# Moving the small transfers of a grouped-query attention backward kernel from POOL's DMA queue to the sync engine's

## The chip, the cores and the metric

The kernel runs on one core of a Trainium2 chip. The metric is the device time of one execution in microseconds (us). Every run used here was in the fast state, with a mean granted TensorE clock of 0.98 to 1.00 except where a text says otherwise. Engines: PE multiplies matrices, DVE and ACT work on vectors, POOL is the general engine, and SP is the sync engine, which here only issues transfers. In the traces a transfer issued by SP or ACT stands in a hardware DMA queue (q1, q10), one issued by POOL in the software one (q0). A ring is the list of transfers that such a queue has on one DMA engine. A transfer lands when the last of its completion signals has come.

## The reference

Forward and backward of softmax attention, 32 batches, 32 query heads on 4 key heads, 4 queries, 2048 keys, head size 128, bf16.

```python
def _fwd_reference(q, k, v):               # q 32x32x4x128, k and v 32x4x2048x128
    k = jnp.repeat(k, Hq // Hkv, axis=1); v = jnp.repeat(v, Hq // Hkv, axis=1)
    scores = jnp.einsum("bhqd,bhkd->bhqk", q, k) * D ** -0.5
    return jnp.einsum("bhqk,bhkd->bhqd", _softmax(scores), v)

def reference(q, k, v, grad_out):
    out, vjp = jax.vjp(_fwd_reference, q, k, v)
    return (out, *vjp(grad_out))           # out, dq, dk, dv
```

Per batch this is 2 MB each of k, v, dk and dv, and 32 KB each of q, grad_out, out and dq.

## The kernel before

The work of a batch is cut into units. A table gives each unit a planned time; units are sorted by it, and each engine runs its own in that order. The names that matter: LQ loads q and grad_out; LK and LV load k and v in transfers of 1 MB; DVs and DKs store dv and dk, 1 MB each; Os and DQs store out and dq; Oe and DQe are the copies that make out and dq in SBUF; QT and VT are PE's transposes of q and v.

```python
PERIOD = 21.3
PLACE = dict(LQ=[-47.936], LK=[-16.977, -14.467], LV=[3.599, 0.95], QT=[-7.484], ...  # cut
    Oe=[18.672], Os=[94.455], DQe=[52.911], DQs=[136.569], ...)                        # cut
SHIFT = {0: dict(LQ=[-769.808], ..., DQs=[-81.021], ...), ...}   # first and last batches; cut
# planned time of a unit: b * PERIOD + PLACE[name] + SHIFT
...
    sm_pool = pool("small", 4)              # four buffers for each name: q, go, o, dq, ...
...
        if name == "LQ":
            t["q"] = sm_pool.tile([P, D], BF16, name="q_sb")
            nc.gpsimd.dma_start(out=t["q"][:], in_=q_r[b])
            t["go"] = sm_pool.tile([P, D], BF16, name="go_sb")
            nc.gpsimd.dma_start(out=t["go"][:], in_=go_r[b])
        elif name in ("LK", "LV"):
            ...                             # cut; 1 MB a transfer
                nc.sync.dma_start(out=whole[:, h], in_=src[b, g][:, h])
...
        elif name in ("Oe", "DQe"):
            x, by = ("o", "rinv") if name == "Oe" else ("dq", "rs")
            t[x] = sm_pool.tile([P, D], BF16, name=x + "_sb")
            ...                             # cut; on ACT or DVE
        elif name in ("Os", "DQs"):
            nc.gpsimd.dma_start(out=(o_r if name == "Os" else dq_r)[b], in_=t["o" if name == "Os" else "dq"][:])
...
        elif name in ("DVs", "DKs"):
            nc.sync.dma_start(...)          # cut; 1 MB a transfer
```

Of the kernel before, what the change touches and what calls it, by code (L numbers as in the profile page):

```python
# [278 lines left out]
def kernel(  # L279
# [11 lines left out]
    nc = tc.nc  # L291
# [25 lines left out]
    q_r, go_r, o_r, dq_r = rows(q), rows(grad_out), rows(out_0), rows(out_1)  # L317
# [12 lines left out]
    def bank(b, *what, n=1, dt=FP32):  # L330
        i = bank_of[(b, "ps", what[0], n) + what[1:]]
        x = psum[:, QW * i:QW * (i + n)]
        return x if dt is FP32 else x.bitcast(BF16).rearrange("p (c d) -> p c d", d=P)

    def copy16(on, out, in_):
        if on == "ACT":
            nc.scalar.copy(out=out.rearrange("p c d -> p (c d)").bitcast(FP32),  # L337
                           in_=in_.rearrange("p c d -> p (c d)").bitcast(FP32))
        else:
            nc.vector.tensor_copy(out=out, in_=in_)  # L340

    def emit(u):
        b, name, arg = u.key[0], u.key[1], u.key[2:]
        t = T[b]
        if name == "LQ":
            t["q"] = sm_pool.tile([P, D], BF16, name="q_sb")
            nc.gpsimd.dma_start(out=t["q"][:], in_=q_r[b])
            t["go"] = sm_pool.tile([P, D], BF16, name="go_sb")
            nc.gpsimd.dma_start(out=t["go"][:], in_=go_r[b])
        elif name in ("LK", "LV"):  # L350
            g, = arg
            p_, src = (k_pool, k_r) if name == "LK" else (v_pool, v_r)
# [79 lines left out]
        elif name in ("ETe", "DTe"):  # L432
            copy16(u.on, t[(name[:2],) + arg][:], t[(name[:2] + "p",) + arg][:])
        elif name in ("O", "DQ"):
            i, = arg
            if i == 0:
                t[name] = bank(b, name)
            xt, x = ("ET", "V") if name == "O" else ("DT", "K")
            for c in range(4 * i, 4 * i + 4):
                for h in range(NH):  # L440
                    r = slice(32 * h, 32 * h + 32)
                    nc.tensor.matmul(t[name][r, 0:D], lhsT=t[xt, c // 8][:, c % 8, r], rhs=t[x, h][:, c, :],  # L442
                                     start=(c == 0), stop=(c == C - 1), tile_position=(0, 32 * h))
# [3 lines that stand above are left out]
            src = t[name[:-1]][:, 0:D]  # L447
            if u.on == "ACT":
                nc.scalar.activation(out=t[x][:], in_=src, func=ACT.Copy, scale=t[by][:])
            else:  # L450
                nc.vector.tensor_scalar(out=t[x][:], in0=src, scalar1=t[by][:], scalar2=None, op0=ALU.mult)
        elif name in ("Os", "DQs"):
            nc.gpsimd.dma_start(out=(o_r if name == "Os" else dq_r)[b], in_=t["o" if name == "Os" else "dq"][:])
        elif name == "DL":
            t["dl"] = sm_pool.tile([P, 1], FP32, name="delta")
            nc.vector.tensor_tensor_reduce(out=junk[:], in0=t["o"][:], in1=t["go"][:], scale=1.0, scalar=0.0,
                                           op0=ALU.mult, op1=ALU.add, accum_out=t["dl"][:])
        elif name == "DS":
            i, = arg
            if i == 0:  # L460
                t["ds"] = ds_pool.tile([P, Sk], BF16, name="ds_sb")
            w = slice(2 * QW * i, 2 * QW * i + 2 * QW)
            nc.vector.scalar_tensor_tensor(out=t["ds"][:, w], in0=t["DP", i][:], scalar=t["dl"][:],  # L463
                                           in1=t["e"][:, w], op0=ALU.subtract, op1=ALU.mult)
        elif name in ("DV", "DK"):
            i, = arg
            if i == 0:
                for g in range(2):
                    t[name, "out", g] = o_pool.tile([P, 2, C, D], BF16, name=name.lower() + "_sb", tag="out")
            accs = [bank(b, name, i, g, n=2) for g in range(2)]  # L470
            t[name, i] = accs
            lhs, rhs = ("e", "dop") if name == "DV" else ("ds", "qp")
            for j in range(CPQ):
                c = CPQ * i + j
                for g in range(2):
                    r = slice(64 * g, 64 * g + 64)
                    nc.tensor.matmul(accs[g][:, 2 * P * j:2 * P * j + 2 * P], lhsT=t[lhs][r, P * c:P * c + P],  # L477
                                     rhs=t[rhs][r, :, :].rearrange("p h d -> p (h d)"), start=True, stop=True,
                                     tile_position=(64 * g, 0))
        elif name in ("DVe", "DKe"):  # L480
            i, g = arg
            copy = nc.scalar.copy if u.on == "ACT" else nc.vector.tensor_copy
            copy(out=t[name[:2], "out", g][:, :, CPQ * i:CPQ * i + CPQ, :],  # L483
                 in_=t[name[:2], i][g][:].rearrange("p (c h d) -> p h c d", h=2, d=D))
        elif name in ("DVh", "DKh"):
            g, w = arg
            c = slice(C // 2 * w, C // 2 * w + C // 2)
            nc.sync.dma_start(out=(dv_r if name == "DVh" else dk_r)[b, g].rearrange("p h (c d) -> p h c d", d=D)[:, :, c],
                              in_=t[name[:2], "out", g][:, :, c, :])
        elif name in ("DVs", "DKs"):  # L490
            g, = arg
            nc.sync.dma_start(out=(dv_r if name == "DVs" else dk_r)[b, g],
                                in_=t[name[:2], "out", g][:].rearrange("p h c d -> p h (c d)"))

    with tc.manual_schedule():
        for u in order:
            if u.on or not u.eng:
                emit(u)
# [27 lines left out]
```

## Time and profile before

| | before |
|---|---|
| median of 2 runs, us | 693.48 (693.37 to 693.58) |
| span of the profiled run, us | 688.6 |
| PE, DVE, ACT, POOL busy | 90%, 81%, 88%, 30% |
| large transfers, issue to landing, 300 to 600 us | 18.7 to 20.6 us |
| small transfers, the same | 5.7 to 6.2 us |

Such a profile is read from what is never idle. Here these are the 16 DMA engines, and the number to look at next is not how busy a queue is, but how long a transfer waits in it. The lines stand in the prediction below.

### The profile page before, as it was taken

The numbers are of one execution on the slowest core, as the hardware profiler recorded it, in microseconds if no ns is written. First come the engines' busy times: TensorE is split into PE (matmuls) and PEld (weight loads), VectorE is DVE, ScalarE is ACT, GpSimd is POOL, SyncE is SP. The second block draws the span as 40 slices with busy tenths as digits, with TensorE's granted clock in tenths as the row PEclk, the third lists the DMA queues.
The fourth block names the chain that finished last, engine by engine and source line by source line (L and its number), as shares of the span: only waits on it lengthen the run. The fifth ranks groups of instructions, "written<-read, shape, count | busy, mean of one in ns | idle before, by whom it ended". The sixth has DMA issues, their size and how long they took to land.

```text
span 688.6 us, 28403 instructions
## 1 busy us (share of the span) xinstructions
PE 620.1 (90%) x12352; PEld 467.1 (68%) x12352; DVE 558.3 (81%) x776; ACT 604.4 (88%) x921; POOL 208.8 (30%) x426
## 2 busy tenths in 40 slices
PE   5899999999999999999999899998889998989984
PEld 4677677777677777766667666676666766766753
DVE  3788888888889888888788878787787887888885
ACT  2889999999999999998899888899888998888883
POOL 2423321333322233331233321333212333113330
PEclk9999999999999999999999999999999999999998
DMA  9999999999999999999999999999999999999967
GB/s 347 403 413 387 415 414 409 415 415 416 415 416 416 414 416 412 397 407 413 408 409 405 410 412 414 399 398 412 405 412 405 406 401 397 408 403 386 391 260 263
DMA packets 75005, 274.47 MB, mean 399 GB/s; under 512 B 6272, under 2 KB 6272, under 8 KB 74880
## 3 DMA queue, kind: packets, MB, share of 16 engines
q1 hardware_dynamic: 70784, 268.45, 97.6%
q0 software_dynamic: 4096, 4.20, 1.8%
q8 instruction: 96, 1.57, 0.8%
q14 instruction: 29, 0.24, 0.1%
HBM read 136.31 MB, written 136.31 MB: 396 GB/s over the span
## 4 chain that ended last, share of the span: by engine, by line
DMA 55%; PE 22%; ACT 13%; issue 5%; POOL 3%; DVE 2%; SPq 0%; POOLq 0%; DVEq 0%; ACTq 0%
DMA v_sb<-in_v_dram 52%; PE psum L372 10%; PE psum L477 6%; ACT dk_sb L483 4%; ACT dv_sb L483 4%; PE psum L431 3%; DMA out_dram<-dv_sb 2%; ACT e_sb L399 2%; PE psum L442 2%; ACT vt_sb L337 2%; POOL dop_sb_103 L411 1%; PE psum L383 1%; DVE kt_sb L390 1%; ACT kt_sb L337 1%; DMA go_sb<-in_grad_out_dram 1%
## 5 line engine op out<-in xcount | busy, mean ns | idle before, releaser
L483 ACT CAST dk_sb<-psum 128x1024 bf16<-128x1024 f32 x159 | 157.6, 1013 | 25.9 <-PE psum L477 24.5
L483 ACT CAST dv_sb<-psum 128x1024 bf16<-128x1024 f32 x155 | 151.7, 1022 | 13.2 <-PE psum L477 12.4
L372 PE MATMUL psum<-ident,v_sb 128*128 128x128 bf16 x2048 | 147.4, 220 | 16.8 <-DMA v_sb<-in_v_dram 15.3
L372 PEld LDWEIGHTS <-v_sb 128*128 128x128 bf16 x2048 | 117.9, 98 | 56.9 <-issue 32.8
L372 PE MATMUL psum<-ident,k_sb 128*128 128x128 bf16 x2048 | 142.4, 221 | 10.2 <-ACT dk_sb L483 10.2
L372 PEld LDWEIGHTS <-k_sb 128*128 128x128 bf16 x2048 | 121.4, 99 | 27.1 <-issue 24.3
L483 DVE CAST dv_sb<-psum 128x1024 bf16<-128x1024 f32 x101 | 122.8, 1220 | 10.8 <-PE psum L477 10.6
L483 DVE CAST dk_sb<-psum 128x1024 bf16<-128x1024 f32 x97 | 115.9, 1219 | 8.5 <-ACT kt_sb L337 4.5
L337 ACT COPY kt_sb<-psum 128x512 f32<-128x512 f32 x190 | 110.3, 595 | 6.6 <-PE psum L372 5.1
L411 POOL TENSOR_SCALAR dop_sb_103<-go_sb,rinv 32x128 bf16<-32x128 bf16 x64 | 38.5, 602 | 225.4 <-DVE rinv L404 97.3
L411 POOL TENSOR_SCALAR dop_sb_102<-go_sb,rinv 32x128 bf16<-32x128 bf16 x64 | 38.5, 602 | 212.5 <-DVE rinv L404 141.1
L463 DVE SCALAR_TENSOR_TENSOR ds_sb<-psum,delta,e_sb 128x1024 bf16<-128x1024 f32 x64 | 81.9, 1279 | 15.1 <-ACT vt_sb L337 13.5
L337 ACT COPY vt_sb<-psum 128x512 f32<-128x512 f32 x131 | 75.5, 599 | 17.6 <-PE psum L372 16.6
L340 DVE COPY vt_sb<-psum 128x1024 bf16<-128x1024 bf16 x125 | 82.9, 681 | 2.9 <-PE psum L372 2.6
L477 PEld LDWEIGHTS <-e_sb 64*128 64x128 bf16 x1024 | 50.0, 93 | 36.3 <-issue 19.6
L399 ACT ACTIVATE e_sb<-psum,m 128x1024 bf16<-128x1024 f32 x64 | 71.1, 1122 | 2.4 <-DVE kt_sb L390 2.2
L340 DVE COPY kt_sb<-psum 128x1024 bf16<-128x1024 bf16 x66 | 44.9, 685 | 18.8 <-PE psum L372 18.8
L477 PEld LDWEIGHTS <-ds_sb 64*128 64x128 bf16 x1024 | 43.3, 94 | 23.8 <-issue 8.8
L477 PE MATMUL psum<-dop_sb_103,e_sb 64*128 64x256 bf16 x512 | 45.2, 270 | 4.1 <-POOL dop_sb_103 L411 1.6
L477 PE MATMUL psum<-dop_sb_102,e_sb 64*128 64x256 bf16 x512 | 44.9, 270 | 3.2 <-ACT dv_sb L483 0.7
L390 DVE TENSOR_SCALAR_CACHE_REDUCE kt_sb<-psum 128x1024 bf16<-128x1024 f32 x32 | 39.2, 1225 | 9.6 <-issue 7.7
L390 DVE TENSOR_SCALAR_CACHE_REDUCE kt_sb<-psum,m 128x1024 bf16<-128x1024 f32 x32 | 41.1, 1284 | 6.5 <-DVE kt_sb L390 3.9
(83 smaller groups left out, 764.5 us busy)
## 6 DMA issues: line engine op xcount, KB each, us to landing
k_sb<-in_k_dram SPq DMA_DIRECT2D x62, 1024.0 KB, 18.7
v_sb<-in_v_dram SPq DMA_DIRECT2D x62, 1024.0 KB, 19.6
out_dram<-dv_sb SPq DMA_DIRECT2D x62, 1024.0 KB, 19.0
out_dram<-dk_sb SPq DMA_DIRECT2D x62, 1024.0 KB, 18.8
k_sb<-in_k_dram SPq DMA_DIRECT2D x4, 512.0 KB, 5.4
v_sb<-in_v_dram SPq DMA_DIRECT2D x4, 512.0 KB, 9.4
out_dram<-dv_sb SPq DMA_DIRECT2D x4, 512.0 KB, 7.9
out_dram<-dk_sb SPq DMA_DIRECT2D x4, 512.0 KB, 6.7
```

The costliest lines, as they stand in the source:

```text
L337: nc.scalar.copy(out=out.rearrange("p c d -> p (c d)").bitcast(FP32), in_=in_.rearrange("p c d -> p (c d)").bitcast(FP32))
L340: nc.vector.tensor_copy(out=out, in_=in_)
L372: nc.tensor.transpose(out=ps[:, j, :], in_=t[x, h][:, 8 * i + j, :], identity=ident[:])
L383: nc.tensor.matmul(t[name, i][r, QW * w:QW * w + QW], lhsT=t["qdt"][:, side, r], rhs=t[x, h, i][:, CPQ * w:CPQ * w + CPQ, :], start=True, ...
L390: nc.vector.tensor_scalar(out=spent, in0=t["S", i][:], scalar1=-scale, scalar2=t["m"][:] if i else None, op0=ALU.mult, op1=ALU.min, accum_ ...
L399: nc.scalar.activation(out=t["e"][:, 2 * QW * i:2 * QW * i + 2 * QW], in_=t["S", i][:], func=ACT.Exp, bias=t["m"][:], scale=scale, accum_o ...
L411: nc.gpsimd.tensor_scalar(out=t["dop"][r, h % 2, :], in0=t["go"][r, :], scalar1=t["rinv"][r, :], scalar2=None, op0=ALU.mult)
L431: nc.tensor.transpose(out=ps[:, j, :], in_=src[:, P * c:P * c + P], identity=ident[:])
L442: nc.tensor.matmul(t[name][r, 0:D], lhsT=t[xt, c // 8][:, c % 8, r], rhs=t[x, h][:, c, :], start=(c == 0), stop=(c == C - 1), tile_positio ...
L463: nc.vector.scalar_tensor_tensor(out=t["ds"][:, w], in0=t["DP", i][:], scalar=t["dl"][:], in1=t["e"][:, w], op0=ALU.subtract, op1=ALU.mult)
L477: nc.tensor.matmul(accs[g][:, 2 * P * j:2 * P * j + 2 * P], lhsT=t[lhs][r, P * c:P * c + P], rhs=t[rhs][r, :, :].rearrange("p h d -> p (h ...
L483: copy(out=t[name[:2], "out", g][:, :, CPQ * i:CPQ * i + CPQ, :], in_=t[name[:2], i][g][:].rearrange("p (c h d) -> p h c d", h=2, d=D))
```

## The change

The intent is to rid POOL of issuing transfers, and to send everything by the hardware path.

```diff
         if name == "LQ":
             t["q"] = sm_pool.tile([P, D], BF16, name="q_sb")
-            nc.gpsimd.dma_start(out=t["q"][:], in_=q_r[b])
+            nc.sync.dma_start(out=t["q"][:], in_=q_r[b])
             t["go"] = sm_pool.tile([P, D], BF16, name="go_sb")
-            nc.gpsimd.dma_start(out=t["go"][:], in_=go_r[b])
+            nc.sync.dma_start(out=t["go"][:], in_=go_r[b])
...
         elif name in ("Os", "DQs"):
-            nc.gpsimd.dma_start(out=(o_r if name == "Os" else dq_r)[b], in_=t["o" if name == "Os" else "dq"][:])
+            nc.sync.dma_start(out=(o_r if name == "Os" else dq_r)[b], in_=t["o" if name == "Os" else "dq"][:])
```

## The prediction

> **What bounds the kernel now.** I read, in this order, the strip of 40 slices, the DMA queues, the chain that ended last, the waits, then the timeline of the queues around 400 us, at the start and at the end.
>
> ```profile
> DMA  9999999999999999999999999999999999999967
> q1 hardware_dynamic: 70784, 268.45, 97.6%
> q0 software_dynamic: 4096, 4.20, 1.8%
> DMA 55%; PE 22%; ACT 13%; issue 5%; POOL 3%; DVE 2%; SPq 0%; POOLq 0%; DVEq 0%; ACTq 0%
> ```
>
> The 16 DMA engines are busy in all but the last two slices, and over half of the last chain is DMA. So **transfers bound the kernel**, not an engine: a batch (21.1 us from 276 us on) moves eight transfers of 1 MB on the sync queue (q1) and four of 32 KB on POOL's queue (q0). What decides is how long each waits in its queue, over 300 to 600 us:
>
> ```profile
> v_sb<-in_v_dram SPq DMA_DIRECT2D x29, 1024.0 KB, 20.6
> out_dram<-dk_sb SPq DMA_DIRECT2D x28, 1024.0 KB, 18.9
> ...
> q_sb<-in_q_dram POOLq DMA_DIRECT2D x14, 32.0 KB, 5.9
> ...
> out_dram<-dq_sb POOLq DMA_DIRECT2D x14, 32.0 KB, 6.2
> ```
>
> The last number is us from issue to landing. A 1 MB transfer takes about 2.6 us of all engines (256 packets of 4 KB, 160 to 164 ns each in the packet records, over 16), so 19 us is a whole batch of transfers queued ahead. The small ones pass that backlog in 6 us, because they stand in another queue. That is what the change takes away.
>
> **What the Trainium skill says.** "DMA: Bandwidth & Descriptors", section "Issuing engines are not separate DMA queues": transfers of all issuers run on the same 16 engines. The trace agrees: packet by packet, at least 16 are active at any time from 100 us on, and when a q0 packet runs, fewer q1 packets do. So the small transfers already cost DMA time, and moving them frees none. Same page, "Queues, rings and completion order": an engine takes turns between rings, and consumes one ring in order. The 6 against 19 us agree. "Perfetto Trace Analysis", section "DMA Instruction — HWDGE (DVE, Sync)": a sync-queue issue waits for its semaphores in the sequencer before it starts, so later issues wait behind it. The first page's "SWDGE vs HWDGE vs iDMA" calls the hardware path the faster to set up; here that matters only where the queue is empty, which it hardly ever is.
>
> **The change, part by part.**
>
> *POOL.* It loses 128 issues of about 0.57 us, 73 us of its 208.8. It is idle 70% of the span; all waits of matmuls on its dop tiles come to 1.6 us. Worth nothing.
>
> *Sync queue, issue.* It gains 128 issues. The program's order per batch b becomes: dv stores, v loads, k load, dk stores, k load, **dq store of b-4, out store of b-2**, q and grad_out loads. The issues already use eight semaphores in turn, and each waits for the landing of the one eight before it: eight in flight at most, exactly one batch today. With twelve per batch, eight in flight are still at least 3 to 5 MB, 8 to 13 us of work, so this limit alone should not empty the engines.
>
> *The order put into the queue.* Both small tiles have four buffers, so the ACT copy that makes dq of b+4 waits until dq of b is stored.
>
> ```profile
> 414.64 0.60 POOL L453 DMA_DIRECT2D out_dram<-dq_sb  x1
> 416.31 2.62 SPq L358 DMA_DIRECT2D k_sb<-in_k_dram  x1
> 423.47 0.37 ACT L449 ACTIVATE dq_sb<-psum,rs 128x128 bf16<-128x128 f32 x1
> ```
>
> Today that store is issued at 414.6 and lands 6.5 us later, 2.4 us before its buffer is needed at 423.5. In the changed order it stands behind the k load, issued until 418.9 and landing about 435.2: 11.7 us late. The same sum gives 5 us late when it first bites (about 196 us), 12 us late from 290 us on. **I do not expect 12 us per batch.** A stalled ACT makes everything later once; then the compute runs that much closer behind the DMA engines, which keep working off the queue, and the pace stays theirs. A check: after the copy, ACT needs 8.8 us until the next dk stores are ready (423.5 to 432.3); behind the dq store stand dv stores, v loads and a k load, 5 MB or 13 us, so the engines do not run dry, with 1 to 2 us to spare. What remains is what the lag costs at the end.
>
> *The end.* The order there puts the last q load (batch 31) directly behind the last v load.
>
> ```profile
> 638.06 4.57 SPq L358 DMA_DIRECT2D v_sb<-in_v_dram  x1
> 650.81 0.22 PE L361 MATMUL psum<-ident,q_sb 128*128 128x128 bf16 x1
> 656.48 0.62 PE L372 MATMUL psum<-ident,v_sb 128*128 128x128 bf16 x8 [1.13 <-DMA v_sb<-in_v_dram]
> ```
>
> That v load lands 20.9 us after issue, at 658.9. The transpose of q, at 650.8 now, must wait for it: 8.1 us. PE waits 1.1 us for v anyway at 656.5, so the end moves by **+7 us**. The lag of the dq stores at this point (7.3 us for batch 23's) is the same time, not an addition.
>
> *The start.* dq of batch 0 is ready only when ACT has made it, yet its store stands ahead of the second dk store:
>
> ```profile
> 41.11 1.25 SPq L492 DMA_DIRECT2D out_dram<-dk_sb  x2
> 48.47 1.29 SPq L492 DMA_DIRECT2D out_dram<-dv_sb  x2
> ...
> 51.58 0.43 ACT L449 ACTIVATE dq_sb<-psum,rs 128x128 bf16<-128x128 f32 x1
> ```
>
> The sync engine would stand from 42.8 to 52.0 us. The backlog is small then: the first dk store lands at 48.9. The other dk store and two dv stores (3 MB) come after 52 instead of 42 and 48.5; the second dk would land at about 59 (52, plus 1.7 for the issues before it, plus 5 for one transfer through an empty queue), the dv stores at 61.5 and 64, the next v load at 66.5 instead of 60.8. From there the engines are full to the end, so the hole is not made good: **+5.7 us**. At the very start q arrives earlier and k 0.8 us later; I count nothing.
>
> *The packets.* Packet records of before: 4 B (a semaphore) 9 ns, 2048 B 84, 4096 B 159. So time is about 9 ns plus 37 ns per KB. Today POOL's queue moves a small transfer in 16 packets of 2 KB, one an engine, 84 ns. The sync queue's packets have the size of one row's piece (4096 and, in the last stores, 2048 B), so I expect 256 B packets, eight an engine: an estimate of 8 x 18.4 = 147 ns. That is +63 ns x 128 = **+8 us**. If they are merged, 0; if short packets cost 30 ns, +20.
>
> *The rate.* 4 KB packets average 160.4 ns from 140 to 260 us, but 162 to 165 from 276 on, with eight always in flight. If fewer MB in flight brings back the lower figure, 2% of 345 us, 6.5 us, returns. I see no cause in the trace, so I take half: **-3 us**.
>
> Sum: 693.5 + 7 + 5.7 + 8 - 3 = 711.2, so **711 us**.
>
> **The rivals.** (1) *Hidden anyway, or a gain*: POOL's work goes, the packets are merged, the rate gets better, the hole at the start closes: 693 to 700. For it: POOL's issues are real work, DMA bytes do not change. Against: POOL bounds nothing, and the backlog of 19 us is plain. (2) *The dq wait recurs each batch*: if its loop (copy, 8.8 us of ACT, issue, 3 MB, landing; together about 20.3 us) turns out longer than the DMA's 21 us, the engines run dry 1 us or more a batch for 24 batches: 735 or more. Against: my sum is 0.7 us under; but that is thin, and gives the range its upper side. (3) *Only the end counts*: packets merged, start covered: 700.
>
> **Range and chances.** Packets (0 to 20), start (3 to 7), end (4 to 9), rate (-6 to 0), dry spells (0 to 8) do not err together: 701 to 725 holds it 8 times in 10. 2% slower begins at 707.3, below my centre but inside the errors of packets and rate: slower 0.69, within 2% 0.29, faster 0.02.
>
> **What would show it.** dq's ACT copy waits for the dq store from about 190 us on, some 10 us the first times together, then under 1 to 2 us a batch; small transfers take 8 to 14 us to land; 1 MB ones fall from 19 to 10 to 14. The wait on v disappears until the end. Sync waits for dq of batch 0 until about 52 us and the DMA strip has a dent there. PE waits for the last q some 8 us, near 660. q1 has 16384 packets of 256 B more. Wrong would be: packets of 2 KB on q1, dents in the DMA strip in mid-run, or a last batch that makes up the lag.

## The result and the profile after

The changed kernel takes **711.59 us** (710.53 to 712.64, 2 runs) against 693.48: a ratio of 1.0274, with a 95% interval of 1.0211 to 1.0337. The ratio is the recorded one, from the fast runs of both kernels in the same rounds; the quotient of the two times shown is 1.0261, so the change costs 18 to 19 us, and with two runs the interval reaches from 14.6 to 23.4. The span of the profiled run went from 688.6 to 708.8 us.

The page of the changed kernel, the DMA strip and its rate in slices of 17.7 us, and the queues:

```profile
DMA  8979999999999999999999999999999999999958
GB/s 335 402 299 344 403 415 412 414 416 415 413 409 367 405 403 404 401 395 400 402 402 391 407 391 400 405 406 394 398 396 397 405 367 383 413 397 415 358 187 324
DMA packets 89341, 274.47 MB, mean 387 GB/s; under 512 B 22656, under 2 KB 22656, under 8 KB 89216
q1 hardware_dynamic: 89216, 272.65, 98.2%
```

The bytes are the same. There are 16384 more packets under 512 B than the 6272 of before: 256 B each, as forecast. The dent is in slices 3 and 4 (35 to 71 us), and there is a small one in slice 13 (213 to 230 us). How long transfers wait, over 300 to 600 us (count, KB, us to landing):

```profile
out_dram<-dk_sb SPq DMA_DIRECT2D x28, 1024.0 KB, 8.7
...
v_sb<-in_v_dram SPq DMA_DIRECT2D x28, 1024.0 KB, 10.7
out_dram<-dq_sb SPq DMA_DIRECT2D x14, 32.0 KB, 11.2
...
q_sb<-in_q_dram SPq DMA_DIRECT2D x13, 32.0 KB, 8.9
```

A small transfer now waits as long as a large one, and the large ones wait half as long as before: the prediction's reason, that the compute runs closer behind and less stands in the queue, is not measured by itself.

The 19 us of before are not a backlog that stands in front of all engines. The trace has 16 completion signals for each transfer, and a landing is the last of them. For the 1 MB transfers from 300 to 600 us the first signal came a median 7.4 us after issue and the last 19.1; 7.4 us of this the last one came alone, behind the other 15. After the change the first came after 6.8 us, and the last 3.9 us later. So nearly all of the shorter wait is that the 16 signals come closer together; why one ran so far behind was not looked into.

The first long wait, in the timeline of ACT (start us, duration us, engine, line, operation, and in brackets the idle time before and what ended it):

```profile
197.17 1.01 ACT L483 CAST dk_sb<-psum 128x1024 bf16<-128x1024 f32 x1 [0.86 <-PE psum L477]
207.64 0.37 ACT L449 ACTIVATE dq_sb<-psum,rs 128x128 bf16<-128x128 f32 x1 [9.45 <-DMA out_dram<-dq_sb]
```

ACT stands 9.5 us at the copy of dq of batch 7 until the store of dq of batch 3 has landed. In the whole run such waits come to 18.6 us in 8 places: one long one, then little ones. At the start, in the timeline of SP:

```profile
41.14 0.38 SPq L492 DMA_DIRECT2D out_dram<-dk_sb  x1
42.80 0.36 SPq L453 DMA_DIRECT2D out_dram<-o_sb  x1
52.06 0.34 SPq L453 DMA_DIRECT2D out_dram<-dq_sb  x1
...
53.41 1.19 SPq L492 DMA_DIRECT2D out_dram<-dk_sb  x1
```

SP stands from 43.2 to 52.1 us before the first dq store, and the second dk store, which was issued at 42 us before, goes out at 53.4. Busy times and rate from 34 to 54 us, of the kernel before and of the changed one, in this order (the last two columns are the busy share of the DMA engines, which can pass 1 where packets overlap, and GB/s):

```profile
34.00:54.00 20.00, 18.40 (x375) 13.73 (x373) 17.43 (x25) 17.91 (x29) 6.37 (x13) 1.00 1.02 412
```

```profile
34.00:54.00 20.00, 18.40 (x376) 13.73 (x373) 17.41 (x25) 17.90 (x29) 4.17 (x9) 1.00 0.74 297
```

The DMA engines lose 28% of 20 us, 5.6 us, while PE, DVE and ACT are as busy as before. At the end, the timelines of SP and PE, one line of each:

```profile
654.20 2.41 SPq L347 DMA_DIRECT2D q_sb<-in_q_dram  x1
...
670.53 0.23 PE L361 MATMUL psum<-ident,q_sb 128*128 128x128 bf16 x1 [1.25 <-DMA q_sb<-in_q_dram]
```

The last q load lands 16.3 us after issue, right behind the last v load, and PE transposes q at 670.5 instead of 650.8.

Two times, read from the trace of each run against the kernel before, tell the causes apart: when the second v load of batches 3 and 31 lands (where the stream of transfers stands), and when dq of batch 31 is copied (where the compute stands). The second minus the first, at batch 31, is called the lag below. In the changed kernel they are +7.7, +11.4 and +18.4 us; the span is +20.2. So 7.7 us are lost before batch 3, 3.7 more by the stream up to batch 31, 7.0 by the compute behind it, and 1.8 after that.

A third figure is the time of the 4 KB packets over their usual 159 ns, summed and divided by 16 engines: the **excess**. It was 17.2 us before and is 21.7 us now. It is a mean over the engines, while a transfer lands with its last signal, so it is a hint and not a price.

Two limits of these figures: each is from one trace, and the trace of the kernel before was a quick execution, with a span of 688.6 us where the timed runs beside the experiments had 689.4 to 692.9. Differences against before that are read from traces can so be some 1 to 4 us too high; compare the runs with each other.

### The profile page after: what moved, and what is told of

It reads as the page before. It is cut to its first block, busy times and chain, and to the rows that moved or that the text cites. A ratio compares the mean times of both kernels' runs of the same rounds, so it can differ in the third digit from the quotient of the medians.

```text
span 708.8 us, 28450 instructions
## 1 busy us (share of the span) xinstructions
PE 626.2 (88%) x12352; PEld 473.1 (67%) x12352; DVE 560.2 (79%) x776; ACT 601.4 (85%) x921; POOL 131.9 (19%) x298
## 4 chain that ended last, share of the span: by engine, by line
PE 44%; ACT 24%; DMA 19%; issue 5%; DVE 4%; POOL 2%; SPq 1%; ACTq 0%; DVEq 0%; POOLq 0%
PE psum L372 19%; DMA out_dram<-dq_sb 14%; PE psum L477 12%; ACT dk_sb L483 9%; PE psum L431 7%; ACT dv_sb L483 5%; ACT e_sb L399 5%; DMA q_sb<-in_q_dram 4%; PE psum L442 3%; ACT vt_sb L337 3%; PE psum L383 2%; DMA v_sb<-in_v_dram 2%; POOL dop_sb L411 2%; DVE kt_sb L390 1%; SPq L358 1%
## 5 line engine op out<-in xcount | busy, mean ns | idle before, releaser
L411 POOL TENSOR_SCALAR dop_sb<-go_sb,rinv 32x128 bf16<-32x128 bf16 x128 | 76.4, 597 | 541.1 <-PE psum L431 405.3
L372 PE MATMUL psum<-ident,v_sb 128*128 128x128 bf16 x2048 | 152.3, 221 | 19.8 <-ACT dq_sb L449 17.8
L372 PEld LDWEIGHTS <-v_sb 128*128 128x128 bf16 x2048 | 120.4, 99 | 61.1 <-issue 54.5
L477 PE MATMUL psum<-dop_sb,e_sb 64*128 64x256 bf16 x1024 | 88.9, 271 | 7.4 <-DVE dv_sb L483 1.5
L477 PE MATMUL psum<-qp_sb,ds_sb 64*128 64x256 bf16 x1024 | 81.1, 271 | 2.4 <-DVE ds_sb L463 1.3
L477 PEld LDWEIGHTS <-e_sb 64*128 64x128 bf16 x1024 | 50.2, 93 | 35.1 <-issue 17.5
L419 POOL TENSOR_SCALAR qp_sb<-q_sb,rinv 32x128 bf16<-32x128 bf16 x128 | 46.9, 366 | 10.5
L431 PE MATMUL psum<-ident,ds_sb 128*128 128x128 bf16 x512 | 39.1, 220 | 10.7 <-ACT e_sb L399 10.7
```

Of the source, the lines that this page charges most:

```text
L372: nc.tensor.transpose(out=ps[:, j, :], in_=t[x, h][:, 8 * i + j, :], identity=ident[:])
L411: nc.gpsimd.tensor_scalar(out=t["dop"][r, h % 2, :], in0=t["go"][r, :], scalar1=t["rinv"][r, :], scalar2=None, op0=ALU.mult)
L419: nc.gpsimd.tensor_scalar(out=t["qp"][r, h % 2, :], in0=t["q"][r, :], scalar1=t["rinv"][r, :], scalar2=scale, op0=ALU.mult, op1=ALU.mult)
L431: nc.tensor.transpose(out=ps[:, j, :], in_=src[:, P * c:P * c + P], identity=ident[:])
L477: nc.tensor.matmul(accs[g][:, 2 * P * j:2 * P * j + 2 * P], lhsT=t[lhs][r, P * c:P * c + P], rhs=t[rhs][r, :, :].rearrange("p h d -> p (h ...
```

## The experiments

Each was a correct kernel, run with three rounds beside the kernel before on the same chip (three chips in all); differences in us come from the ratio times 693. The change itself was timed in another session, with two runs, and an interval of 14.6 to 23.4 us: differences of a few us from it are not clear of noise.

| run | ratio, 95% interval | us over before | v of batch 3 | v of batch 31 | dq of batch 31 | excess, us |
|---|---|---|---|---|---|---|
| the change | 1.0274 (1.0211 to 1.0337) | 19.0 | +7.7 | +11.4 | +18.4 | 21.7 |
| dq_only | 1.0165 (1.0139 to 1.0191) | 11.4 | +5.7 | +9.2 | +15.8 | 22.0 |
| lq_only | 1.0199 (1.0162 to 1.0236) | 13.8 | -0.3 | +5.9 | +15.7 | 19.7 |
| o_only | 1.0025 (1.0008 to 1.0042) | 1.7 | -1.3 | +1.3 | +1.3 | 17.5 |
| start_order | 1.0182 (1.0153 to 1.0211) | 12.6 | +0.6 | +6.1 | +14.7 | 22.6 |
| end_order | 1.0251 (1.0220 to 1.0281) | 17.4 | +8.3 | +13.5 | +18.6 | 23.1 |
| dq6_bufs | 1.0220 (1.0192 to 1.0248) | 15.2 | +9.4 | +7.8 | +14.9 | 17.2 |
| end_both | 1.0087 (1.0064 to 1.0110) | 6.0 | +8.6 | +8.1 | +8.2 | 16.2 |
| all_fixes | 1.0060 (1.0038 to 1.0082) | 4.2 | -0.2 | +5.7 | +5.7 | 20.7 |
| extra_loads | 1.0178 (1.0151 to 1.0205) | 12.3 | +0.6 | +15.7 | +15.7 | 24.3 |
| dq_fixed | 0.9963 (0.9948 to 0.9978) | -2.6 | -0.3 | +0.9 | +0.9 | 18.1 |

### One part of the change at a time

`dq_only`, from the kernel before:

```diff
-            nc.gpsimd.dma_start(out=(o_r if name == "Os" else dq_r)[b], ...)
+            (nc.gpsimd if name == "Os" else nc.sync).dma_start(out=(o_r if name == "Os" else dq_r)[b], ...)
```

> Only the dq stores go to the sync queue; the out stores and the q and grad_out loads stay with POOL. My theory: the hole at the start is due to the first dq store alone (+7.5 us on the landing of the loads from batch 3 on, as in the full change), 32 transfers in short packets cost 32 x 63 ns = +2 us, and the wait of ACT for the dq store puts the compute some 5 to 6 us closer behind the DMA engines at the end: 693.5 + 7.5 + 2 + 5.5 = 708.5 us. Rival A (the end is late only because the last q load stands behind the last v load): no lag at the end, 703 us. Rival B (the loads or out stores make the hole): under 700 us.

The hole at the start came with the dq stores alone, with the 5.7 us that the prediction gave it, and so did the lag at the end (15.8 - 9.2 = 6.6 us). The time was 11.4 us over before, not 15: after the last dq copy the span gained back 3 us (span +12.8). The number happens to be rival A's 703, but its reason, no lag, is not in the trace.

`lq_only`, from the kernel before:

```diff
-            nc.gpsimd.dma_start(out=t["q"][:], in_=q_r[b])
+            nc.sync.dma_start(out=t["q"][:], in_=q_r[b])
-            nc.gpsimd.dma_start(out=t["go"][:], in_=go_r[b])
+            nc.sync.dma_start(out=t["go"][:], in_=go_r[b])
```

> Only the q and grad_out loads go to the sync queue. My theory: no hole at the start (landings of v from batch 3 on within 1.5 us of before), ACT never waits for a dq store, 64 transfers in short packets cost 64 x 63 ns = +4 us, and PE waits some 8 us at the transpose of the last q, which stands behind the last v load: +7. Sum 704.5 us. Rival A (the end is late because of the dq stores alone): 697.5 us. Rival B (a faster first byte of the hardware queue and a freed POOL give something back): under 694 us.

No hole, and no wait for dq, and yet the compute lags 9.8 us at the end (15.7 - 5.9). In the waits of this run (us in total, times, longest):

```profile
PE psum L372 <- DMA v_sb<-in_v_dram: 17.8, 16, 2.0
PE psum L361 <- DMA q_sb<-in_q_dram: 10.3, 4, 4.5
```

PE waits for v in small pieces, as in the kernel before, and for q four times: twice at the start, 4.5 us for the q of batch 29 (at 608 us) and 2.9 us for that of batch 31 (at 665). A q load behind the large transfers does hold PE, but the larger of the two waits is one that the prediction had left out, and its 8 us for the last q are not there. The time was 3 us over the expected 11.

`o_only` is the edit of `dq_only` with the out stores in place of the dq stores.

> Only the out stores go to the sync queue. They stand behind the same transfers as the dq stores, but the buffers of out are needed 10.5 us later in the batch than those of dq: in the kernel before, the transfer ahead would land 1.2 us too late at most, and the first one's wait (until 22.6 us) falls where 8 us of transfers are queued. My theory: no dent at the start, waits of DVE for the out store under 2 us a batch, 32 transfers of short packets 2 to 5 us: 2 to 6 us over before. Rival (any small store behind the large transfers costs what the dq store did): 11 us over before.

It cost 1.7 us, just under the expected 2 to 6; DVE waits 15.2 us for out stores, in 6 places of up to 3.2 us, more than the 2 us expected. The three parts alone sum to 26.9 us, the whole change is 19. They overlap: two of them lead to a lag, 6.6 us (`dq_only`) and 9.8 us (`lq_only`), and the whole change has 7.0, not their sum.

### Two causes, one lag

`dq6_bufs` and `end_order`, each from the changed kernel:

```diff
+    od_pool = pool("od", 6)
-            t[x] = sm_pool.tile([P, D], BF16, name=x + "_sb")
+            t[x] = (od_pool if x == "dq" else sm_pool).tile([P, D], BF16, name=x + "_sb")
```

```diff
# SHIFT of the last batch
-        LQ=[53.318], ...
+        LQ=[-5.9], ...
```

> The full change, with six buffers for dq instead of four, so that the dq store has 42 us more to land before its buffer is needed. My theory: ACT's wait for the dq store goes (18.6 us in 8 waits after the change, to under 2), the compute runs ahead until it waits for v again as before, and yet the time hardly moves, 709 to 711.5 us, because the hole at the start stays and at the end the last q load behind the last v load holds PE by itself (some 8 us there). Rival (the dq wait is what makes the end late): 704 us.

> The full change, with the last q and grad_out loads (batch 31) moved up to stand right behind those of batch 29, some 50 us earlier. My theory: the wait of PE for the last q goes (2.5 us there after the change), but the lag from the dq stores stays, so the time falls by no more than that: 709 to 711 us. Rival (the last q load is what makes the end late): 704 us.

With six buffers no wait for a dq store is left in the waits. What PE waits for then, in all and twice near the end:

```profile
PE psum L362 <- DMA q_sb<-in_q_dram: 12.0, 4, 5.9
```

```profile
611.29 0.29 PE L362 MATMUL psum<-ident,q_sb 128*128 128x128 bf16 x1 [5.92 <-DMA q_sb<-in_q_dram]
...
667.01 0.23 PE L362 MATMUL psum<-ident,q_sb 128*128 128x128 bf16 x1 [1.89 <-DMA q_sb<-in_q_dram]
```

(L362 is the transpose of q; one line was added above it. The first is that of batch 29, the second that of batch 31; the other two waits are at the start.) The lag at the end is still 7.1 us (14.9 - 7.8), and it comes with batch 29's q: the dq copy of batch 25 is 8.7 us late, that of batch 27, copied after that transpose, 15.9. The time fell by 3.8 us, which is within the noise, and the excess from 21.7 to 17.2, one trace each. Moving only the last q load brought 1.6 us, no more than noise, a lag of 5.1 us stayed, and so did ACT's waits for dq stores:

```profile
ACT dq_sb L449 <- DMA out_dram<-dq_sb: 26.5, 13, 10.1
```

(The 2.5 us that the expectation gives to the last q are the wait for the first q, at 2.5 us; in the changed kernel the last q held PE for 1.25 us.)

`end_both` has six buffers, the move of batch 31's loads, and a like move of batch 29's (`LQ=[36.086]` to `LQ=[14.736]`).

> The full change, with six buffers for dq and with the q and grad_out loads of batches 29 and 31 moved up by about one and three batches. Six buffers alone and the move of batch 31's loads alone had each taken off less than 4 us (15.5 and 17.5 us over before, against 18 to 19). My theory: they are two causes of the same lag, so that only both together take it off: 7 to 9 us over before, which is the hole at the start, and the compute at the end lags the landing of the last v load no more than before. Rival (they add up, each its own few us): 13 to 14 us over before.

It is 6.0 us over before, a bit under the expected 7 to 9. The dq copy of batch 31 and the v load of batch 31 are now late by the same 8 us, so the lag is gone: 7.0 us in the change, 7.1 without the dq wait, 5.1 without batch 31's q, 0.1 here. Alone, the two edits took off 3.8 and 1.6 us; all edits together took off 13. This is the strongest result: **one wait hid the other**. With the dq wait, the q of batch 29 lands 3 us before PE comes to it (614.1 and 617.3 us in the changed kernel), because the compute is late already; without it, PE waits 5.9 us for that q. The second cause is thus more batch 29's q load than batch 31's, the one that was moved alone. Batch 29's loads were not tried by themselves, so the shares of the 13 stay open.

### The hole at the start

`start_order`, from the changed kernel, and `all_fixes`, from `end_both`:

```diff
# SHIFT of batch 0: the first dq store goes behind two dv stores and a v load
-        DQe=[1.892], DQs=[-81.021], ...
+        DQe=[1.892], DQs=[-70.5], ...
```

> The full change, with the first dq store (batch 0) moved down behind the two dv stores and the first v load of batch 3 in the sync queue's order. My theory: the sync engine no longer stands until 52 us, the dent in the DMA strip goes, and since the DMA engines are full from there to the end, the whole 7.5 us of later landings (v of batch 3 in the changed kernel against before) come off the total: 18 us over before becomes 10 to 11 us over before. Rival (the engines make the hole good later in any case): 16 to 18 us over before.

> The full change, with the hole at the start and both causes at the end taken away: first dq store moved down, six buffers for dq, q and grad_out loads of batches 29 and 31 moved up. What remains is the short packets in the sync queue: predicted 8 us, but the landings of v in the run with six dq buffers grew by nothing from batch 3 to 31, so I now expect less, 1 to 5 us over before. Rival A (the prediction's 8 us for the packets): 8 us over before. Rival B (a part is still unnamed): over 10.

The dent goes. The DMA strips of `start_order` and of `end_both`, which keeps the hole, in this order:

```profile
DMA  8999999999999999999999999999999999999848
```

```profile
DMA  8988999999999999999999999999999989999988
```

The landing of v of batch 3 came back from +7.7 to +0.6. The time came down by 6.4 us in `start_order`, to 12.6 over before, between its expectation (10 to 11) and its rival (16 to 18); with the noise of the change this can be nearly the whole hole. But from `end_both` to `all_fixes`, in the same rounds, it came down by only 1.8. In `all_fixes`, v is on time at batch 3 and 5.7 us late at batch 31; in `end_both` it is 8.6 us late at both. In `all_fixes` the 4 KB packets have 4.5 us more excess than in `end_both` (20.7 against 16.2), most of it in the loads of k and v. So in this pair most of what the hole takes is given back later, with faster packets. Why the packets get slower without the hole is not settled, and each excess is from one trace. `all_fixes` at 4.2 us (2.6 to 5.7) is within its own expectation (1 to 5); so all that is left, the short packets included, costs less than the prediction's 8 us. Not all waits are gone there: DVE waits 23.9 us for out stores, in 9 places.

### The short packets by themselves

`extra_loads`, from the kernel before:

```diff
+    scr_pool = pool("scr", 2)
                 nc.sync.dma_start(out=whole[:, h], in_=src[b, g][:, h])
+            if name == "LK" and g == 1 and b > 0:
+                for side in (q_r, go_r):
+                    extra = scr_pool.tile([P, D], BF16, name="scr_sb")
+                    nc.sync.dma_start(out=extra[:], in_=side[b])
```

> The kernel before, with two more loads of 32 KB per batch (q and grad_out once more, into a tile that nobody reads) on the sync queue, 62 in all; POOL's transfers stay. This measures short packets on the sync queue by themselves, with no wait attached. By the packet records (8 packets of 18 ns and a semaphore of 9 ns on each engine) it costs 62 x 0.156 = 9.7 us, if these times add up one after the other; if they overlap their neighbours by some 5 ns each, as a semaphore's seems to, 62 x 0.11 = 7 us. Rival (short packets fit into gaps of the engines): under 2 us.

It cost 12.3 us, over both estimates, and v of batch 31 landed 15.7 us late. The excess of the large packets grew by 7.1 us. Without it, 8.6 us by the landing or 5.2 by the time are left, 0.14 or 0.08 us for each of 62 transfers; the estimates were 0.156 and 0.11. So short packets do take engine time, and added ones are not hidden; but they came with slower large packets, which I had not expected, and how much of the cost is which stays open.

### A clean version, and another queue

`dq_fixed` is `dq_only` with six buffers for dq and the first dq store moved down.

> Only the dq stores go to the sync queue, with six buffers for dq and the first dq store moved down. My theory: the 11.5 us of the run with only the dq stores were the hole and the lag; without both, 32 transfers of short packets are left, 2 to 5 us over before. Rival (the transfers themselves cost it): 9 us or more.

It is the **fastest kernel**: 691.02 us (690.55 to 691.54, 4 runs) beside 693.43 for the kernel before, 0.4% less. The size is small and below the 2% line, but the interval is clear of 1. The dq store now lands late and nobody waits for it. The issues of this run from 300 to 600 us:

```profile
out_dram<-dk_sb SPq DMA_DIRECT2D x28, 1024.0 KB, 18.6
...
out_dram<-dq_sb SPq DMA_DIRECT2D x14, 32.0 KB, 16.7
```

It had been expected 2 to 5 us slower. Where its 2.6 us come from stays open: its trace (span 689.5) is a typical run of it, that of the kernel before (688.6) is quicker than any of its timed runs here (691.3 to 692.3), so the two traces cannot tell.

`dq_act` and `all_act` send the dq stores alone, or all four small transfers, to ACT's hardware queue (`nc.scalar.dma_start`).

> Only the dq stores move, to ACT's hardware queue instead of the sync queue: the same hardware path and the same short packets, but another ring, with nothing ahead in it. My theory (what costs is standing behind the large transfers and in the sync engine's order): they land in 3 to 7 us, ACT never waits for one, there is no dent at the start; ACT spends 0.4 us on each issue, 13 us in all, mostly within its idle 12%: 2 to 6 us over before. Rival (the hardware path or its packets cost it): 11 us over before, as with the sync queue.

> All four small transfers go to ACT's hardware queue. My theory: they land in 3 to 7 us, no wait for a dq store, no hole, no wait for the last q; but ACT, which works 19 of 21.1 us a batch and paced the batches at 20.25 us before the DMA engines did, gets 4 issues of 0.4 us or more a batch: 21.9 us a batch, so it is ACT that bounds, 12 to 25 us over before. Rival (issues hide in ACT's idle time): the packets alone, 4 to 8 us over before.

Both fell far outside: 789.81 us (ratio 1.1367, granted clock 0.93) and 791.56 us (1.1412, 0.93). The stores land as fast as I said, but look at where ACT issues them. One issue in ACT's timeline in `dq_act` (start, duration, engine, line):

```profile
421.15 0.34 ACTq L453 DMA_DIRECT2D out_dram<-dq_sb  x1
```

The view of waits of the same run (who waits for what: total us, number of waits, longest in us):

```profile
ACT dq_sb L449 <- DMA out_dram<-dq_sb: 93.4, 21, 6.0
```

And the view of its dq tile, from issue to landing:

```profile
DMA to landing us min/median/max: 3.1/6.3/8.2
```

In ACT's own order the store of batch b-4 stands just ahead of the copy of batch b that needs its buffer. POOL and SP ran ahead of that point; ACT cannot, since it is the engine that waits. So it issues the store and then stands for its landing, 4.4 us on average, in each of batches 7 to 27: 93.4 us in 21 waits, about the 93 us by which the span grew (781.3). This is the wait that recurs each batch, which the prediction feared for the sync queue and did not find there. The landing of 6.3 us (5.5 to 6.1 for the stores issued from 51 to 128 us, before the waits begin and while the DMA engines are full) shows that the hardware path and its short packets are not what makes dq late on the sync queue, but its place behind the large transfers. In `all_act` ACT stands as long at the same copy, 56.2 us put down to dq stores and 37.3 to out stores. So neither expectation was tested: what ACT's issues would cost without the wait stays open.

## Why the prediction was right

The mechanism held: transfers bound the kernel, and the loss is the order in the queue, at the start and at the end. That 711 and 711.6 agree so closely is luck. By the traces the start cost 7.7 us (5.7 forecast), the end 8.8 (7), packets and rate together 3.7 (8 - 3 = 5); the measured 711.6 itself is known to some 4 us.

- **Transfers bound, POOL is worth nothing.** Right for the first. POOL's busy time fell from 208.8 to 131.9 us, and no run shows a gain that can be put down to it; the 2.6 us of `dq_fixed` have no cause yet. The reading behind it was a little too strong: in the trace of before, fewer than 16 packets were active in 1.7% of the time from 100 to 600 us, so not "at least 16" at any time, and of its 19 us 7.4 were the wait for the last of 16 signals, so no backlog before all engines.
- **The dq wait shifts once and does not recur.** Right, and the central step. It was 9.5 us at batch 7, then small ones, 18.6 us in all; 24 times 12 would have been 290. "The engines do not run dry" held nearly: in slice 13, at the long wait, the rate fell to 367 GB/s, but v landed no later after it than at batch 3 (+7.7 there, +6.3 at batch 13).
- **The end, +7.** Right in size for the compute (7.0), with 1.8 more after it. Also right that the dq lag and the late q are the same time: `dq_only` and `lq_only` each have the lag, and `end_both` shows it gone. But PE's wait "some 8 us" for the last q did not come: it was 1.25 us at 670.5, since the dq lag had already made the compute late, and without that lag it is batch 29's q that holds PE most (5.9 us in `dq6_bufs`).
- **The start, +5.7.** The hole was found where forecast, and measured 7.7 us at batch 3 (5.7 in `dq_only`). The step that failed is "the engines are full to the end, so the hole is not made good": in `all_fixes` against `end_both`, v of batch 3 landed 8.8 us earlier and the time fell by 1.8.
- **The packets, +8.** The form was right, 256 B at 18.1 ns against the estimate of 18.4. The net cost was too large: `all_fixes`, with all of the short packets, is 4.2 us over before. `extra_loads` puts an added transfer at 0.08 to 0.14 us; POOL's transfers, which cost time too (84 and 9 ns on each engine), went away in exchange.
- **The rate, -3.** Wrong in sign. Fewer MB in flight did not bring the 160 ns packets back: from 300 to 600 us 4 KB packets took 166.0 ns after the change, 163.5 before, and the engines moved 396 GB/s against 407. I had "no cause in the trace" and should have given the term no centre but zero.

## What to carry to other kernels

A queue is an order, not only a path: before a small transfer is put behind large ones, compare, for each batch, when the transfer ahead of it lands and when its buffer or data is needed, at the start and at the end as well as in the middle. If it is late, deepen the buffer or move the issue earlier; then the move is harmless, as with the dq stores here. And when two waits lead to the same lag, removing one can show next to nothing, so remove both before calling either free.

## What the Trainium skill lacked or had wrong

- "DMA: Bandwidth & Descriptors", section "Issuing engine by pattern", sends simple loads and stores to the sync engine and calls its path generally faster. In the runs the sync engine's path was the faster one only where its queue was empty: the first q load landed in 1.8 us from the sync engine, in 4.7 us from POOL; behind large transfers it took 8.9 us (median, 300 to 600 us) against 5.9.
- The same page, section "Queues, rings and completion order", gives 9 to 17 descriptors as typical of a packet. It does not say that this depends on the issuer: rows of 256 B went as packets of 256 B (18 ns) from the sync engine's and ACT's queues, and as packets of 2048 B (84 ns) from POOL's.
- The same page, section "Rules for kernel authors", says that spreading transfers over issuers only saves issue time. No run here tests that for bandwidth. What it lacks, though it follows from the turns between rings that the page describes, is that a ring of its own spares a small transfer the backlog of another (6 against 16.7 us for the dq store with full queues); nor does it say that an engine which both issues a store and needs its buffer next waits for the landing itself (`dq_act`: 93.4 us in 21 waits).
- No page of those read tells why 4 KB packets take longer than their usual 159 ns for part of a run. That excess was 16 to 24 us in the runs on the sync queue and POOL's, 17.2 before, and its cause is open. Nor does one give the size of what one late completion signal adds to a landing: a median 7.4 us before the change, 0.3 after it.
